# Retention and two MLPs on one core: scores as 64 by 64 products, three chunk buffers in turn, first weights behind chunks 8 and 11

## The chip, the cores and the metric

The kernel runs on one core of a Trainium2 chip. The metric is the device time in microseconds (us) of one execution. Three runs of the kernel before gave 571.97, 572.69 and 572.76 us, a median of 572.69. The profile that is read here is one further execution of 573.28 us, of which the traced span is 571.5 us; the other 1.78 us lie around the span.

## The reference

A retention layer with a decay per head goes into two MLPs with different activations. Cut to what matters:

```python
gamma = 1 - 2 ** (-5 - arange(8))          # one decay per head
for t in range(768):                       # B, H, S, D = 2, 8, 768, 64
    state = gamma * state + einsum('bhd,bhe->bhde', k[:, :, t], v[:, :, t])
    y[:, :, t] = einsum('bhd,bhde->bhe', q[:, :, t], state) / sqrt(64)
x = y as [1536 tokens, 512]
h = x @ w_in;  x = (h * tanh(softplus(h))) @ w_out     # first MLP, 512 -> 2048 -> 512
h = x @ w_in2; out = (h * cos(h)) @ w_out2             # second MLP, same sizes
```

q, k and v are float32; the four weights are float64 and are taken apart on the chip into a high and a low float32 part.

## The kernel before, in words

**Two stages.** The retention runs first, in 12 chunks of 128 tokens (six for each of the two batches). Behind it come the two MLPs, 24 steps of matrix products with 512 moving columns. TensorE goes from the one to the other without a break.

**One chunk of the retention.** Chunk g arrives as two loads of 512 KB on the SP queue (`chunk_loads`, `att_load`): columns 0 to 1023 hold q and k (here "qk half"), columns 1024 to 2047 hold v and the other layout of k ("vk half"). Four groups of products run on TensorE:

- `att_scores` (line 325): 8 products, key by query, per head; 64 rows by 128 columns of the array, in float32. It writes two PSUM tiles, which VectorE masks into `p` (`att_mask`).
- `att_inter` (line 370): 8 products of 64 rows by 64 columns, the state of the chunk before (`st`) with the decayed queries (`qd`).
- `att_update` (line 341): 8 products of 128 rows by 64 columns, which add the chunk (`vd`) to the state. The last chunk of a batch (5 and 11) has none.
- `att_out` (line 381): 8 products of 128 rows by 64 columns, masked scores by v.

Each float32 product is two records (weight load and matmul) in the trace, so a group of 8 products is "x16". The first chunk of a batch (0 and 6) has no `att_inter`.

**Order on TensorE.** It is written by hand: scores(0), a few products with zeros, and then for n = 0 to 11: scores(n+1), inter(n), update(n), out(n). Behind out(11) come the first products of the MLP (`products(11)`, `deal`), line 428.

**The other engines in this stage.** POOL makes `qd` and some `vd`; ScalarE the other `vd` (lists `VD_ACT`), some states `st` (`ST_ACT`) and the high part of x (`att_x_high`); VectorE the masks, the other states and the low part of x.

**The planner.** `Plan` puts every operation in order by costs and dependences written in the kernel. TensorE and SP keep the written order; on the other engines what can start first comes first. `op(..., uses=, new=)` names the buffers that an operation reads or takes.

**Where the chunks lie.** Chunks 0 and 1 lie in a tile of x, 2 to 4 in three buffers `qkv`, 5 to 7 in the three buffers of the output weights, 8 and 9 in two buffers of g, and 10 and 11 in the buffers of chunks 2 and 3. So no load of chunks 2 to 9 waits for a chunk's end.

**First weights.** The weight tile `("i", 0, 0)` of the first MLP is loaded in two halves (here i00a and i00b), `("i", 0, 1)` in two more (i01a, i01b). In the written order of SP i00a stands behind chunk 6, i00b behind chunk 9, and i01a and i01b behind chunk 11. Each half is then taken apart: abs (ScalarE, `w_abs_act`), clamp, exponent, sign (VectorE), high part (ScalarE), low and low part (VectorE). `hold` keeps single steps of this from coming before a named step of the retention.

Of the kernel before, what the change touches and what calls it, by code (L numbers as in the profile page):

```python
# [10 lines left out]
F32 = mybir.dt.float32  # L11
# [13 lines left out]
BLK = 512  # L25
# [7 lines left out]
IN_WO = (5, 6, 7)  # L33
IN_G = (8, 9)
# [142 lines left out]
def retention_two_mlps(ctx: ExitStack, tc: tile.TileContext, qkv, w1i, w1o, w2i, w2o, consts, out):  # L177
# [89 lines left out]
    att = {}  # L267
    vd = {}
# [12 lines left out]
    def att_load(g, lo, hi, eng=nc.sync):  # L281
        if not att:
            t = x_p.tile([128, 2, KD, BLK], F32R, tag="x", name="qkv")
            for n in range(2):
                att[n] = t[:, n].rearrange("p a b -> p (a b)").bitcast(F32)
        elif g in IN_WO and g not in att:
            t = wo_p.tile([128, 2, 2, 512], F32R, tag="wo", name="qkv")
            att[g] = t.rearrange("p a b c -> p (a b c)").bitcast(F32)
        elif g in IN_G and g not in att:
            t = g_p.tile([128, 2, 2, BLK], F32R, tag="g", name="qkv")  # L290
            att[g] = t.rearrange("p a b c -> p (a b c)").bitcast(F32)
        elif g not in att:
            att[g] = att_p.tile([128, 2048], F32, tag="qkv", name="qkv", bufs=3)
        eng.dma_start(out=att[g][:, lo:hi], in_=qkv[g, :, lo:hi])  # L294
# [24 lines left out]
    def att_scores(g):  # L319
        qk = qk_of(g)  # L320
        ss = [ps_p.tile([128, NPAIR, C], F32, tag="s", name="ps_s", bufs=3) for _ in range(2)]
        for a in range(NPAIR):
            for e in range(2):
                h = slice(D * e, D * e + D)
                nc.tensor.matmul(ss[e][:, a, :], qk[h, a, 1, :], qk[h, a, 0, :], start=True, stop=True)  # L325
# [255 lines left out]
    def chunk(g):  # L581
        return ("qkv", max(g, 1))

    def chunk_loads(g, cuts, queue=nc.sync):
        key = chunk(g)
        for lo, hi in zip(cuts, cuts[1:]):
            n = op(
                "SP", (hi - lo) * (0.00142 if g < 3 else 0.00122), att_load, g, lo, hi, queue,
                uses=[key], new=None if key in plan.owner else (key, 3, "x" if g < 2 else "wo" if g in IN_WO else "g" if g in IN_G else "qkv"),
# [5 lines left out]
    def chunk_pre(g):  # L595
        c = g % NCH
        key = chunk(g)
        on_act = g in VD_ACT
        if c + 1 < NCH:
# [3 lines left out]
                    new=None if part else (("vd", g), 2), uses=[key, ("vd", g)],  # L603
# [3 lines left out]
        if c > 0:  # L607
            name, cost, eng = ("DVE", 0.72, nc.vector) if g in QD_DVE else ("POOL", 1.95, nc.gpsimd)
            at["qd", g] = op(
                name, cost, att_qd, g, eng, needs=at["qk", g] + at["decq"], new=(("qd", g), 2), uses=[key]  # L610
# [5 lines left out]
    def chunk_scores(g):  # L616
        s = [("s", g, e) for e in range(2)]
        first = op(None, 0.0, nothing, new=(s[0], 3, "s"))
        at["s", g] = op("PE", 1.05, att_scores, g, needs=at["qk", g] + [first], new=(s[1], 3, "s"), uses=[chunk(g), s[0]])
# [315 lines left out]
```

## Time and profile before

| | us |
|---|---|
| median of three runs | 572.69 |
| profiled execution | 573.28 |
| its span | 571.5 |
| TensorE busy (matmul) in the span | 565.8 |
| VectorE / ScalarE / POOL busy | 382.6 / 230.1 / 97.5 |
| retention, to the first MLP product | 45.65 |

The rows that the prediction rests on stand in a section of their own below. PE is TensorE's matmuls, PEld its weight loads, DVE VectorE, ACT ScalarE, POOL GpSimd, SP the queue that issues the loads. In a timeline, neighbouring instructions of one line are merged: start, length, engine, line, and the count; a bracket gives the idle time ahead and what ended it. A matmul's end in the trace is modelled, so starts are read, and the time of a group of products is taken from its start to the start of the next group. The granted TensorE clock is 1.0 of full speed (2.4 GHz) in all 40 slices of the page.

### The profile page before, as it was taken

The page shows a single profiled execution, that of the slowest core. Times are in us where ns is not written, and L with a number is a line of the kernel's source. Part 1 is how long each engine was busy: PE and PEld are TensorE (multiplying, and loading weights), DVE is VectorE, ACT ScalarE, POOL GpSimd, SP SyncE. Part 2 cuts the span into 40 slices and gives each one's busy share as a digit, 9 for nine tenths or more (in the row PEclk, how much of TensorE's full clock was granted, in tenths as well). Part 3 has the DMA queues.
Part 4 walks back from the last instruction along what each step waited for, and adds up shares of the span by engine and source line. Part 5 has one row for each costly group of instructions (what it writes and reads, how often), then busy time and mean ns, then how long its engine had stood idle before and what let it go on. Part 6 is the DMA issues. An engine that isn't in the chain of part 4 may idle for free.

```text
span 571.5 us, 7260 instructions
## 1 busy us (share of the span) xinstructions
PE 565.8 (99%) x3054; PEld 468.4 (82%) x3054; DVE 382.6 (67%) x416; ACT 230.1 (40%) x284; POOL 97.5 (17%) x74
## 2 busy tenths in 40 slices
PE   8999999999999999999999999999999999999997
PEld 6888888888888888888888888888888888888886
DVE  5779889662375427653487985898498894765462
ACT  3574543422303303214326465465345354354240
POOL 6680001111110301111101111032010312010000
PEclk9999999999999999999999999999999999999999
DMA  8982254422032200412021030304004010000113
GB/s 297 413 335 75 75 210 158 147 75 73 1 131 91 73 1 0 148 73 75 0 75 73 26 123 1 138 10 147 1 0 148 32 41 2 1 1 1 73 38 110
DMA packets 14721, 49.91 MB, mean 87 GB/s; under 512 B 1632, under 2 KB 2016, under 8 KB 14688
## 3 DMA queue, kind: packets, MB, share of 16 engines
q1 hardware_dynamic: 14688, 49.44, 23.4%
q8 instruction: 24, 0.39, 0.3%
q14 instruction: 9, 0.07, 0.0%
HBM read 46.29 MB, written 3.15 MB: 86 GB/s over the span
## 4 chain that ended last, share of the span: by engine, by line
PE 94%; DMA 4%; SPq 1%; ACT 0%; issue 0%; DVE 0%; ACTq 0%
PE ps_h L428 46%; PE ps_o L451 46%; DMA qkv<-qkv_dram 4%; SPq L294 1%; PE ps_y L381 1%; PE ps_y L370 1%; PE ps_s L325 1%; PE ps_u L341 0%; ACT vd L308 0%; ACT x L395 0%; DVE acc L517 0%; SPq L758 0%; ACT st L353 0%; ACTq L308 0%
## 5 line engine op out<-in xcount | busy, mean ns | idle before, releaser
L428 PE MATMUL ps_h<-x,wi 128*128 128x512 f32 x1152 | 264.8, 389 | 0.0
L428 PEld LDWEIGHTS ps_h<-x,wi 128*128 128x128 f32 x1152 | 216.1, 188 | 45.0 <-issue 0.2
L451 PE MATMUL ps_o<-wo,g 128*128 128x512 f32 (+1 forms) x588 | 132.5, 385 | 0.0
L451 PE MATMUL ps_o<-g,wo 128*128 128x512 f32 x576 | 132.3, 389 | 0.0
L451 PEld LDWEIGHTS ps_o<-wo,g 128*128 128x128 f32 x588 | 108.9, 188 | 22.1
L451 PEld LDWEIGHTS ps_o<-g,wo 128*128 128x128 f32 x576 | 108.1, 188 | 22.5
L494 DVE TENSOR_TENSOR g<-mish,g 128x1024 fp32r<-128x1024 f32 x24 | 33.4, 1393 | 59.2 <-ACT g L490 59.2
L262 POOL TENSOR_TENSOR wo<-mag,wo 128x1024 fp32r<-128x1024 f32 x14 | 35.8, 2557 | 212.8 <-ACT wo L248 212.8
L510 DVE TENSOR_TENSOR acc<-ps_o,acc 128x1024 f32<-128x1024 f32 x35 | 42.8, 1222 | 34.6 <-PE ps_o L451 34.4
L262 POOL TENSOR_TENSOR wi<-mag,wi 128x1024 fp32r<-128x1024 f32 x12 | 30.3, 2525 | 193.1 <-ACT wi L248 193.1
L461 ACT ACTIVATE mish<-ps_h 128x1024 f32<-128x1024 f32 (+1 forms) x25 | 24.9, 995 | 95.1 <-PE ps_h L428 95.1
L474 DVE SCALAR_TENSOR_TENSOR turns<-whole,turns 128x1024 f32<-128x1024 f32 x24 | 29.4, 1223 | 44.7 <-ACT whole L470 44.7
L466 ACT ACTIVATE turns<-ps_h,quarter 128x1024 f32<-128x1024 f32 x24 | 26.7, 1114 | 65.4 <-PE ps_h L428 65.1
L239 DVE SCALAR_TENSOR_TENSOR mag<-raw,mag 128x1024 uint32<-128x1024 uint32 (+1 forms) x38 | 42.2, 1110 | 1.1
L483 ACT ACTIVATE turns<-turns 128x1024 f32<-128x1024 f32 x24 | 25.5, 1062 | 34.8 <-DVE turns L480 34.6
L494 DVE TENSOR_TENSOR g<-turns,g 128x1024 fp32r<-128x1024 f32 x24 | 33.2, 1384 | 8.0 <-ACT g L490 8.0
L486 DVE TENSOR_TENSOR turns<-turns,ps_h 128x1024 f32<-128x1024 f32 x24 | 29.2, 1216 | 10.1 <-ACT turns L483 6.8
L254 DVE SCALAR_TENSOR_TENSOR mag<-raw,mag 128x1024 uint32<-128x1024 uint32 x26 | 33.7, 1301 | 0.4
L490 ACT CAST g<-turns 128x1024 fp32r<-128x1024 f32 x24 | 25.1, 1044 | 16.9 <-DVE turns L486 16.9
L248 ACT CAST wi<-mag 128x1024 fp32r<-128x1024 f32 (+1 forms) x20 | 17.5, 876 | 27.3 <-DVE mag L254 22.4
L470 ACT ACTIVATE whole<-turns,magic 128x1024 f32<-128x1024 f32 x24 | 27.7, 1153 | 0.8
L480 DVE TENSOR_SCALAR turns<-turns 128x1024 f32<-128x1024 f32 x24 | 27.0, 1126 | 0.8
(50 smaller groups left out, 330.2 us busy)
## 6 DMA issues: line engine op xcount, KB each, us to landing
qkv<-qkv_dram SPq DMA_DIRECT2D x24, 512.0 KB, 10.1
raw<-w1i_dram SPq DMA_DIRECT2D x16, 512.0 KB, 4.2
raw<-w1o_dram SPq DMA_DIRECT2D x16, 512.0 KB, 4.1
raw<-w2i_dram SPq DMA_DIRECT2D x16, 512.0 KB, 4.0
raw<-w2o_dram SPq DMA_DIRECT2D x16, 512.0 KB, 3.6
out_dram<-acc SPq DMA_DIRECT2D x11, 256.0 KB, 2.1
out_dram<-acc SPq DMA_DIRECT2D x2, 128.0 KB, 1.7
few<-consts_dram SPq DMA_DIRECT2D x1, 146.0 KB, 2.2
```

The lines of the kernel that those rows point to most:

```text
L239: nc.vector.scalar_tensor_tensor(out=a, in0=high, scalar=0xC0000000, in1=a, op0=ALU.bitwise_and, op1=ALU.bitwise_or)
L254: nc.vector.scalar_tensor_tensor(out=w_all_of(it, single)[:, ns], in0=raw_t[it][:, ns, :, 0], scalar=29, in1=mag_t[it][:, ns], op0=ALU.log ...
L262: eng.tensor_sub(out=w[:, :, 1], in0=w_all_of(it, single)[:, ns].bitcast(F32), in1=w[:, :, 0].bitcast(F32))
L428: nc.tensor.matmul(h[:, 0 if h_tag(k) == "s" else f % 2, :], w[:, f % 2, a, kk * 128 : (kk + 1) * 128], x[:, b, kk, :], start=(a + b + kk ...
L451: nc.tensor.matmul(ps, lhs, rhs, start=(n == 0), stop=(n == 3 * GF - 1))
L466: nc.scalar.activation(out=t_t[k], in_=h_t[k], func=AF.Identity, scale=INV_2PI, bias=quarter)
L470: nc.scalar.activation(out=n_t[k], in_=t_t[k], func=AF.Identity, bias=magic)
L474: nc.vector.scalar_tensor_tensor(out=t, in0=n_t[k], scalar=MAGIC, in1=t, op0=ALU.subtract, op1=ALU.subtract)
L480: nc.vector.tensor_scalar(out=t, in0=t, scalar1=-0.5, scalar2=0.5, op0=ALU.max, op1=ALU.min)
L486: nc.vector.tensor_mul(out=t_t[k], in0=t_t[k], in1=h_t[k])
L494: nc.vector.tensor_sub(out=g[:, :, 1, :], in0=t_t[k], in1=g[:, :, 0, :].bitcast(F32))
L510: nc.vector.tensor_add(out=acc, in0=o_t[m * NG + G, j, p], in1=acc)
```

## The change

- **Scores.** Each of the 8 score products is split by its 128 keys into two of 64 rows by 64 columns: 16 products, in the order (rows 0, keys 0), (rows 1, keys 0), (rows 0, keys 1), (rows 1, keys 1) for each pair of heads.
- **Buffers.** Chunks 0 and 1 stay in the tile of x; from chunk 2 on the chunks take three buffers a0, a1, a2 in turn (`HOME`). So the load of chunk g waits for chunk g-3, from chunk 5 on: its qk half for the readers of that chunk's qk half (scores, qd), its vk half for those of the vk half (vd, update, out). The buffers of the output weights and of g hold no chunk any more.
- **First weights.** In SP's order i00a stands behind chunk 8, i00b behind chunk 11 and ahead of i01a.
- **Holds.** Clamp and sign of i00a wait for the masks of chunks 8 and 9 (were 6 and 7); the clamp of i00b waits for the mask of chunk 11 (was 9), its abs for x of chunk 9 (was 6).
- The planner's costs of scores and inter are 0.94 and 0.55 (were 1.05 and 0.62); they order operations and are no measurement.

```diff
--- before.py
+++ after.py
@@ -30,8 +30,7 @@
 GF = 4
 NG = NF // GF
 NCHK = B * NCH
-IN_WO = (5, 6, 7)
-IN_G = (8, 9)
+HOME = ("x0", "x1", "a0", "a1", "a2", "a0", "a1", "a2", "a0", "a1", "a2", "a0")
 H_ATT = {(0, 0, 0): "s", (0, 1, 0): "h0", (0, 0, 1): "y", (0, 1, 1): "h0"}
 VD_ACT = (1, 2, 4, 7, 9)
 ST_ACT = (3, 4, 6, 7, 8, 9)
@@ -265,6 +264,7 @@
 
     x_t = {}
     att = {}
+    homes = {}
     vd = {}
     qd = {}
     state = {}
@@ -279,18 +279,15 @@
         return x_t[m, j]
 
     def att_load(g, lo, hi, eng=nc.sync):
-        if not att:
-            t = x_p.tile([128, 2, KD, BLK], F32R, tag="x", name="qkv")
-            for n in range(2):
-                att[n] = t[:, n].rearrange("p a b -> p (a b)").bitcast(F32)
-        elif g in IN_WO and g not in att:
-            t = wo_p.tile([128, 2, 2, 512], F32R, tag="wo", name="qkv")
-            att[g] = t.rearrange("p a b c -> p (a b c)").bitcast(F32)
-        elif g in IN_G and g not in att:
-            t = g_p.tile([128, 2, 2, BLK], F32R, tag="g", name="qkv")
-            att[g] = t.rearrange("p a b c -> p (a b c)").bitcast(F32)
-        elif g not in att:
-            att[g] = att_p.tile([128, 2048], F32, tag="qkv", name="qkv", bufs=3)
+        home = HOME[g]
+        if g not in att:
+            if home == "x0" and home not in homes:
+                t = x_p.tile([128, 2, KD, BLK], F32R, tag="x", name="qkv")
+                for n in range(2):
+                    homes[f"x{n}"] = t[:, n].rearrange("p a b -> p (a b)").bitcast(F32)
+            elif home not in homes:
+                homes[home] = att_p.tile([128, 2048], F32, tag=home, name="qkv", bufs=1)
+            att[g] = homes[home]
         eng.dma_start(out=att[g][:, lo:hi], in_=qkv[g, :, lo:hi])
 
     def qk_of(g):
@@ -320,9 +317,13 @@
         qk = qk_of(g)
         ss = [ps_p.tile([128, NPAIR, C], F32, tag="s", name="ps_s", bufs=3) for _ in range(2)]
         for a in range(NPAIR):
-            for e in range(2):
-                h = slice(D * e, D * e + D)
-                nc.tensor.matmul(ss[e][:, a, :], qk[h, a, 1, :], qk[h, a, 0, :], start=True, stop=True)
+            for t in range(2):
+                keys = slice(D * t, D * t + D)
+                for e in range(2):
+                    h = slice(D * e, D * e + D)
+                    nc.tensor.matmul(
+                        ss[e][keys, a, :], qk[h, a, 1, keys], qk[h, a, 0, :], start=True, stop=True, skip_group_check=True,
+                    )
         s_t[g] = ss
 
     def att_mask(g, e):
@@ -578,15 +579,16 @@
             for n in range(ns.start, ns.stop):
                 at["w", it, n] = last
 
-    def chunk(g):
-        return ("qkv", max(g, 1))
+    def chunk(g, part):
+        return [(part, g)] + [("qkv", "x")] * (HOME[g][0] == "x")
 
     def chunk_loads(g, cuts, queue=nc.sync):
-        key = chunk(g)
         for lo, hi in zip(cuts, cuts[1:]):
+            half = "qk" if lo < 1024 else "vk"
+            key = chunk(g, half)
             n = op(
-                "SP", (hi - lo) * (0.00142 if g < 3 else 0.00122), att_load, g, lo, hi, queue,
-                uses=[key], new=None if key in plan.owner else (key, 3, "x" if g < 2 else "wo" if g in IN_WO else "g" if g in IN_G else "qkv"),
+                "SP", (hi - lo) * (0.00142 if g < 3 else 0.00122), att_load, g, lo, hi, queue, uses=key,
+                new=None if key[0] in plan.owner else (key[0], 1, half + HOME[g]),
             )
             for part, last in (("qk", 1024), ("v", 1536), ("k", 2048)):
                 if lo < last and hi > last - 512:
@@ -594,20 +596,19 @@
 
     def chunk_pre(g):
         c = g % NCH
-        key = chunk(g)
         on_act = g in VD_ACT
         if c + 1 < NCH:
             at["vd", g] = [
                 op(
                     *(("ACT", 0.98) if on_act else ("POOL", 1.15)), att_vd, g, part, needs=at["v", g] + at["dec"],
-                    new=None if part else (("vd", g), 2), uses=[key, ("vd", g)],
+                    new=None if part else (("vd", g), 2), uses=[*chunk(g, "vk"), ("vd", g)],
                 )
                 for part in range(2 if on_act else 1)
             ]
         if c > 0:
             name, cost, eng = ("DVE", 0.72, nc.vector) if g in QD_DVE else ("POOL", 1.95, nc.gpsimd)
             at["qd", g] = op(
-                name, cost, att_qd, g, eng, needs=at["qk", g] + at["decq"], new=(("qd", g), 2), uses=[key]
+                name, cost, att_qd, g, eng, needs=at["qk", g] + at["decq"], new=(("qd", g), 2), uses=chunk(g, "qk")
             )
 
     def nothing():
@@ -616,7 +617,7 @@
     def chunk_scores(g):
         s = [("s", g, e) for e in range(2)]
         first = op(None, 0.0, nothing, new=(s[0], 3, "s"))
-        at["s", g] = op("PE", 1.05, att_scores, g, needs=at["qk", g] + [first], new=(s[1], 3, "s"), uses=[chunk(g), s[0]])
+        at["s", g] = op("PE", 0.94, att_scores, g, needs=at["qk", g] + [first], new=(s[1], 3, "s"), uses=[*chunk(g, "qk"), s[0]])
         for e in range(2):
             at["p", g, e] = at["p", g] = op(
                 "DVE", 0.71, att_mask, g, e, needs=[at["s", g]] + at["mask"],
@@ -630,7 +631,7 @@
         u, st = ("u", g // NCH), ("st", g)
         at["u", g] = op(
             "PE", 0.52, att_update, g, needs=at["vd", g] + at["k", g] + ([at["st", g - 1]] if c else []),
-            uses=[u, chunk(g), ("vd", g)], new=None if c else (u, 1, "u"),
+            uses=[u, *chunk(g, "vk"), ("vd", g)], new=None if c else (u, 1, "u"),
         )
         at["st", g] = op(
             *(("ACT", 1.0) if g in ST_ACT else ("DVE", 0.43)), att_state, g, needs=[at["u", g]], new=(st, 2), uses=[u],
@@ -639,11 +640,11 @@
     def chunk_inter(g):
         if g % NCH:
             uses = [("st", g - 1), ("qd", g), ("y", g)]
-            op("PE", 0.62, att_inter, g, needs=[at["st", g - 1], at["qd", g]], uses=uses, new=(("y", g), 1, y_tag(g)))
+            op("PE", 0.55, att_inter, g, needs=[at["st", g - 1], at["qd", g]], uses=uses, new=(("y", g), 1, y_tag(g)))
 
     def chunk_out(g):
         y, x = ("y", g), ("x", 0, g // 4)
-        uses = [("p", g), chunk(g), y]
+        uses = [("p", g), *chunk(g, "vk"), y]
         at["y", g] = op(
             "PE", 0.98, att_out, g, needs=[at["p", g]] + at["v", g], uses=uses,
             new=None if y in plan.owner else (y, 1, y_tag(g)),
@@ -795,13 +796,12 @@
 
     at["close"] = op(None, 0.0, close)
     op("PE", 5.5, start_up)
+    op(None, 0.0, nothing, new=(("qkv", "x"), NJ, "x"))
     load = op("SP", 0.4, load_consts, new=("few", 3, "g"))
     cuts = (0, 1024, 2048)
-    for g in range(7):
+    for g in range(9):
         chunk_loads(g, cuts)
-    weight(("i", 0, 0), lambda: [chunk_loads(g, cuts) for g in (7, 8, 9)])
-    for g in (10, 11):
-        chunk_loads(g, cuts)
+    weight(("i", 0, 0), lambda: [chunk_loads(g, cuts) for g in (9, 10, 11)])
     weight(("i", 0, 1))
     plan.given.remove("SP")
     last = op("DVE", 0.85, att_mask_grow, needs=[load], uses=["few"])
@@ -840,13 +840,13 @@
 
     i00, i01 = ("i", 0, 0), ("i", 0, 1)
     for n, what, ns, it in (
-        (6, "clamp", 0, i00), (7, "sign", 0, i00), (11, "dve low", 0, i00),
-        (9, "clamp", 1, i00), (11, "dve low", 1, i00),
+        (8, "clamp", 0, i00), (9, "sign", 0, i00), (11, "dve low", 0, i00),
+        (11, "clamp", 1, i00), (11, "dve low", 1, i00),
     ):
         hold(at[what, it, ns], at["p", n])
     hold(at["sign", i00, 1], at["xl", 9])
     hold(at["act", i00, 0], at["xh", 4])
-    hold(at["act", i00, 1], at["xh", 6])
+    hold(at["act", i00, 1], at["xh", 9])
     hold(at["high", i00, 1], at["st", 10])
     hold(table, at["xh", 10])
     hold(at["act", i01, 0], at["xl", 10])
```

## Rows read from the trace of the kernel before

**Rows 1.** The page: busy us, share of the span, instructions; busy tenths in 40 slices.

```profile
PE 565.8 (99%) x3054; PEld 468.4 (82%) x3054; DVE 382.6 (67%) x416; ACT 230.1 (40%) x284; POOL 97.5 (17%) x74
...
DMA  8982254422032200412021030304004010000113
```

**Rows 2.** The chain that ended last, 0 to 80 us: start, length, what.

```profile
17.44 11.76 DMA qkv<-qkv_dram
...
45.72 32.89 PE ps_h L428 x144
```

**Rows 3.** Timeline of PE: start, length, engine, line, operation, count.

```profile
12.46 1.16 PE L325 MATMUL ps_s<-qkv 64*128 64x128 f32 x16
13.55 0.67 PE L370 MATMUL ps_y<-qd,st 64*64 64x128 f32 x16
14.15 0.69 PE L341 MATMUL ps_u<-vd,qkv 128*64 128x64 f32 x16
14.67 1.04 PE L381 MATMUL ps_y<-p,qkv 128*64 128x128 f32 x16
15.64 1.16 PE L325 MATMUL ps_s<-qkv 64*128 64x128 f32 x16
...
45.65 14.60 PE L428 MATMUL ps_h<-x,wi 128*128 128x512 f32 x63
```

**Rows 4.** Timeline of PEld (weight loads), 12.4 to 15.7 us.

```profile
12.46 0.97 PEld L325 LDWEIGHTS ps_s<-qkv 64*128 64x128 f32 x16 [0.32 <-DMA qkv<-qkv_dram]
13.55 0.42 PEld L370 LDWEIGHTS ps_y<-qd,st 64*64 64x64 f32 x16
14.15 0.55 PEld L341 LDWEIGHTS ps_u<-vd,qkv 128*64 128x64 f32 x16 [0.17 <-ACT vd L308]
14.61 0.86 PEld L381 LDWEIGHTS ps_y<-p,qkv 128*64 128x64 f32 x16
```

**Rows 5.** Timeline of PE, cut at 13.82 and at 13.93 us: the same group.

```profile
13.55 0.45 PE L370 MATMUL ps_y<-qd,st 64*64 64x128 f32 x8
...
13.55 0.56 PE L370 MATMUL ps_y<-qd,st 64*64 64x128 f32 x12
```

**Rows 6.** Timeline of PE, 26.8 to 33 us.

```profile
26.87 1.09 PE L381 MATMUL ps_y<-p,qkv 128*64 128x128 f32 x16
28.05 1.16 PE L325 MATMUL ps_s<-qkv 64*128 64x128 f32 x16
...
30.63 1.16 PE L325 MATMUL ps_s<-qkv 64*128 64x128 f32 x16
32.07 0.99 PE L370 MATMUL ps_y<-qd,st 64*64 64x128 f32 x16 [0.28 <-ACT st L353]
```

**Rows 7.** Timeline of ACT, 29 to 47 us.

```profile
29.28 1.06 ACT L308 ACTIVATE vd<-qkv,cst 128x64 f32<-128x64 f32 x4 [1.93 <-DMA qkv<-qkv_dram]
...
31.68 0.90 ACT L353 ACTIVATE st<-ps_u,cst 128x64 f32<-128x64 f32 x4
...
46.62 0.62 ACT L248 CAST wi<-mag 128x512 fp32r<-128x512 f32 x1
```

**Rows 8.** Windows: stretch, busy us of PE, PEld, DVE, ACT, POOL; PEclk, DMA share, GB/s.

```profile
20.00:23.00 3.00, 3.00 (x64) 2.63 (x64) 1.89 (x3) 2.71 (x10) 2.69 (x5) 1.00 1.02 410
...
41.00:44.00 3.00, 3.00 (x64) 2.56 (x64) 2.37 (x5) 0.56 (x2) 1.58 (x3) 1.00 0.04 18
```

**Rows 9.** Timeline of SP: the last loads of chunks issued.

```profile
26.72 4.09 SPq L294 DMA_DIRECT2D qkv<-qkv_dram  x4
```

**Rows 10.** Issue to landing: line 211 at 48 to 53 us (two halves), then line 294.

```profile
DMA to landing us min/median/max: 3.3/3.8/4.2
...
DMA to landing us min/median/max: 4.9/10.1/12.0
```

**Rows 11.** Timeline of POOL: qd of chunk 2.

```profile
13.36 1.53 POOL L316 TENSOR_TENSOR qd<-qkv,cst 64x256 f32<-64x256 f32 x2
```

**Rows 12.** Waits of PEld from 45 us to the end: us in total, times, longest.

```profile
PEld ps_h L428 <- issue: 0.2, 1, 0.2
```

## Prediction

> **What bounds the kernel now.** I read the page first: TensorE is busy for 99% of the span, the other engines for 67% or less [rows 1]. Then the chain that ended last: a load of a chunk up to 29.2 us, then TensorE without a break, with the first MLP product at 45.7 us [rows 2]. Behind 45 us TensorE's weight loads wait 0.2 us in all [rows 12]: the MLPs are one unbroken run on TensorE, and whatever the retention ends sooner reaches the end one for one, as long as nothing in the MLPs' first steps comes late. So only the time from the first chunk to 45.65 us is in play.
>
> In that stage a chunk is a slot of four groups on TensorE, 12.46 to 15.64 us: scores 1.09, inter 0.60, update 0.52, out 0.97, together 3.18 us [rows 3]. At 12.46 us TensorE still waited for a load [rows 4]; nothing can be gained ahead of that. Behind it, it is TensorE's own pace but for two late starts. Scores of chunk 7 start 1.18 us behind the start of out(5), where 1.02 would do (0.97, and 0.05 for the change of form, below): 0.16 late. Inter(7) starts 1.44 us behind scores(8), where 1.09 would do: 0.35 late, behind a state that ScalarE makes after it stood 1.93 us for the vk half of chunk 7 [rows 6, 7]. The loads run ahead at 410 GB/s with the DMA engines full [rows 8], so 512 KB take 1.28 us and a chunk 2.56.
>
> **Scores, and the inter behind them.** Inter is the nearest row to a product of 64 by 64 with 128 columns. Cut at 13.82 us the group holds 8 records and ends at 14.00, cut at 13.93 it holds 12 and ends at 14.11 [rows 5], and all 16 end at 14.22 [rows 3]: four records, that is two products, per 0.11 us. Its 0.60 are 4 x 0.11 and 0.16 at its edges. Weight loads show the edges: inter's end at 13.97 and update's begin at 14.15, 0.18 later, while out's begin (14.61) before update's end (14.70) [rows 4]. Update and out have one form, inter and update have not; scores and inter have not either (loads end 13.43, begin 13.55). I put 0.05 of the 0.16 at the start and 0.11 at the end.
>
> The new scores are 16 products, 8 x 0.11 = 0.88. They come behind out, of another form, so 0.05 more: 0.93. Inter behind them has the same form and loses its start, 0.55. The pair takes 1.48 where it took 1.69: 0.21 less. The other bound: in the new order every second neighbour uses the same columns of the array, in inter none does. If that delays one group of two products by 0.11, the pair takes 1.59, 0.10 less; and if the split saves nothing at all, 0. I take 0.19, near inter, since the engine, the form and the number of columns are inter's. Behind 12.46 us there are nine such pairs (scores 2 to 6 and 8 to 11), and scores(7), behind which an update comes, saves 0.05. Sum: 9 x 0.19 + 0.05 = 1.76 us. The slot becomes 2.99 us.
>
> **The three buffers.** Before, the last chunk loads were issued at 26.7 to 30.8 us, far ahead [rows 9]. Now the vk half of chunk g+2 waits for out(g-1). All of SP's queue stands behind that wait: the qk half of g+3, and later the weights. A half that is issued alone lands 3.3 us later, and one issued 0.4 behind it took 4.2 [rows 10]; so the next is some 1.28 behind. So the qk half of g+3 is there 3.35 + 1.28 = 4.6 us after out(g-1) ends. TensorE asks for it two slots later, 5.98 us. In the steady state the wait is covered with 1.4 us to spare; half vk has over 2 us more. At the start, chunk 5: its qk half waits for qd(2), which POOL ends at 14.89 us [rows 11]; the queue of loads is then still full, and it lands near 20, for scores(5) at 21.4. Cost nil; without that cover each us of lateness would be one us of TensorE per slot.
>
> **Where it isn't covered.** Chunk 5 has no update and chunk 6 no inter, so slots are short there, and i00a now stands between vk8 and qk9. Let out(4) end at U.
> - vk7 lands at U + 3.4; in the profile it took 2.9 us from such a landing (29.2) to inter(7) (32.07), over vd and the state on ScalarE [rows 6, 7]. So inter(7) can start at U + 6.3. TensorE gets there at U + 0.93 + 0.55 + 1.02 + 1.04 + 0.52 + 0.97 + 0.93 = U + 5.96: 0.34 late, as before (0.35).
> - vk8 waits for out(5), which ends at U + 2.50. With i00a ahead of it qk9 lands 0.05 + 3.35 + 2 x 1.28 = 5.96 later, at U + 8.46. TensorE gets to scores(9) at U + 6.3 + 0.55 + 0.52 + 0.97 = U + 8.34: 0.1 late.
>
> That is 0.45 of new lateness for 0.51 of old. It counts on idle DMA engines. Before, a few per cent of the engines' time went on at 41 to 44 us, 0.04 x 16 = 0.6 of one engine [rows 8]: one engine runs late, and a half has landed when the last of 16 engines has. I take 0.35 us of that into the wait for chunk 9; the bounds are 0 and 0.7. Net of the late starts: +0.3.
>
> **Edits with one answer.** The old buffers of chunks 5 to 9 are free sooner, which nothing waits for [rows 12]. i00b lands behind vk11, which waits for out(8), now ending near 36.4: 36.5 + 3.35 + 1.28 = 41.1 us. Its high part needs abs, clamp, exponent, sign and cast, some 2.9 us by their lengths in the trace, so 44.0 at best; it is wanted when 12 products (12 x 0.23 us) of the first half are through, near 46.9. Before, the cast stood at 46.62, ahead of a need at 48.4 [rows 7]. The cover is 2 to 3 us of those products; if VectorE's masks push the chain further than that, TensorE waits for the rest.
>
> **Sum.** 1.76 - 0.3 = 1.46: the first MLP product near 44.2 us. The profiled execution would go from 573.28 to 571.8; it lies 0.59 above the median, so the median goes from 572.69 to 571.2.
>
> **Rivals.**
> - *A, as above*, 571.2. With the pair at 0.21 less, no late engine and no wait at inter(7), the gain is 2.4 (570.3); with 0.10 and the full 0.7, it is 0.95 + 0.05 - 0.65, about 0.35 (572.3). Chance 0.63.
> - *B, the loads set the pace.* If a half lands L after its release, two slots can't be shorter than L + 1.28. At L = 4.7 the cover is gone, at L = 5.1 the slot is 3.18 again: 572.2 to 573.2. For it: halves in a full queue took 4.9 to 12 us [rows 10]. Against: the queue is empty when a load waits for its buffer. The case that the split saves nothing counts here too (about 572.5). Chance 0.22.
> - *C, slower: the small products go one at a time.* Scores, update and out, whose neighbours share rows or columns of the array, take one product per 0.11 to 0.14 us with 128 columns; only inter, whose neighbours share neither, takes two per 0.11 [rows 3, 5]. If sharing is what counts, 16 products take 16 x 0.11 = 1.78: the pair is 0.64 longer, nine times, and the other scores 0.69: 6.4 us, 579. It turns to a loss when a product costs over (1.69 - 0.55) / 16 = 0.071 us. Against: the rates also fit the share of the array that a product fills, halves for those three and quarters for inter, and the new ones fill quarters. Chance 0.12.
> - *D, slower: a price per instruction.* 16 more records per chunk at inter's 0.0275 us each are 0.44, eleven times, 4.8 us: 577.5. Against: these 0.0275 are inter's whole time per record, so there is no room for a price on top. Chance 0.03. The Trainium skill, TensorEngine Tiling, "Instruction Overhead", states about 60 cycles of overhead for each matmul and warns of tiling a small dimension further; as an estimate from that page, 16 x 25 ns would be 0.4 us more per chunk.
>
> **How the numbers follow.** About 0.2%, 1.15 us (571.54), is what a measurement of this kernel can tell from no change. A's centre is only 0.35 beyond it, and its spread 0.6, so some 0.7 of A is faster and the rest no change. Faster 0.46, same 0.38, slower 0.16 (C, D, a little of B). The range takes in A and B with the runs' 0.4: 570.0 to 573.1.
>
> **What would show it.** Right: scores to inter 0.93, inter to update 0.55, slots of 3.0 us, no weight-load pause between scores and inter, first MLP product at 44 to 44.5. SP shows waits for out(g-3); PE a wait of 0.3 to 0.8 at scores(9) and one at inter(7). Wrong: scores near 1.8 (C) or 1.35 (D); waits for loads at every scores from chunk 6 on (B); a wait behind 45.65 for i00b.

## The result and the profile after

The kernel after takes 576.3 us in the median (four runs, 575.46 to 577.35), the kernel before beside it 572.4; the ratio is 1.0069, 95% interval 1.0048 to 1.0091. It is slower by 3.9 us where 1.5 us less was forecast. The profiled execution took 575.65 us with a span of 573.7, 2.2 more than the span of before; the granted clock is 1.0 in all slices, as before.

The timeline of PE of the kernel after, from the first scores of the stretch to the MLP (start, length, engine, line, operation, count; in the bracket the idle time ahead and what ended it):

```profile
15.61 1.09 PE L324 MATMUL ps_s<-qkv 64*64 64x128 f32 x30 [0.36 <-DMA qkv<-qkv_dram]
...
18.66 1.10 PE L324 MATMUL ps_s<-qkv 64*64 64x128 f32 x32
19.58 0.62 PE L371 MATMUL ps_y<-qd,st 64*64 64x128 f32 x16
20.13 0.50 PE L342 MATMUL ps_u<-vd,qkv 128*64 128x64 f32 x9
20.91 0.39 PE L342 MATMUL ps_u<-vd,qkv 128*64 128x64 f32 x6 [0.27 <-issue]
...
30.68 0.87 PE L324 MATMUL ps_s<-qkv 64*64 64x128 f32 x20
32.29 0.54 PE L324 MATMUL ps_s<-qkv 64*64 64x128 f32 x10 [0.74 <-issue]
...
35.79 1.10 PE L324 MATMUL ps_s<-qkv 64*64 64x128 f32 x32 [0.92 <-DMA qkv<-qkv_dram]
...
37.78 0.28 PE L382 MATMUL ps_y<-p,qkv 128*64 128x128 f32 x1
38.73 1.09 PE L382 MATMUL ps_y<-p,qkv 128*64 128x128 f32 x15 [0.68 <-issue]
...
47.30 3.03 PE L429 MATMUL ps_h<-x,wi 128*128 128x512 f32 x12
50.56 11.63 PE L429 MATMUL ps_h<-x,wi 128*128 128x512 f32 x50 [0.23 <-ACT wi L247]
```

Set it against [rows 3]. Scores and inter take 18.66 to 20.13 = 1.47 us where they took 1.69: the products themselves gained what was forecast. But the groups are now broken in the middle. A group of one kind, whose inputs are all there, stops after 9 of 16 records of update(3), after 20 of 32 of scores(8), after one of out(8), and what ended the pause is "issue": no engine and no DMA that the profile knows of. A fourth such break stands in scores(6), where the weight loads stand still for 0.33 us, and loads come late, most of all that of scores(9) at 35.79. The first MLP product is at 47.30 us, 1.65 later than in [rows 3], and the MLP itself has a break at 50.56, where it waits for a weight.

The account from the scores of chunk 2 to the MLP (12.46 to 45.65 = 33.19 us before, 12.21 to 47.30 = 35.09 after), each pause as the time by which the broken group and the one behind it, which it draws out, are longer than in a slot without a pause:

| | us |
|---|---|
| before | 33.19 |
| old lateness gone: scores(7) 0.16, inter(7) 0.35 at its start and 0.32 in itself | -0.83 |
| nine pairs shorter by 0.22, scores(7) by 0.05 | -2.03 |
| pauses: update(3) 0.54, scores(6) 0.40, scores(8) 1.16, out(8) 0.99 | +3.09 |
| loads late: scores(3) 0.53 with the pair behind it, scores(7) 0.14, scores(9) 0.99 | +1.66 |
| sum (measured 35.09) | 35.08 |

The 0.32 in inter(7) of before is read from its start at 32.07 [rows 6] to that of the group behind it, 0.92 where 0.60 would do:

```profile
32.99 0.69 PE L341 MATMUL ps_u<-vd,qkv 128*64 128x64 f32 x16
```

With half a microsecond more at 50.56 (the twelve products of the first half would have ended at 50.06) this is the 2.2 us of the spans. The other three runs of after were 0.2 shorter to 1.7 us longer than its profiled one, the runs of before lay within 0.8, so the medians differ by more than the two traces. One execution of another kernel, the small products below, took 2041.6 us and is counted nowhere.

From the page of after, the busy row and a DMA queue (transfers, MB, share of 16 engines):

```profile
PE 564.8 (98%) x3246; PEld 467.7 (82%) x3246; DVE 382.1 (67%) x416; ACT 230.3 (40%) x284; POOL 97.0 (17%) x74
...
q8 instruction: 25, 0.41, 0.3%
```

q8 is the queue that the page calls "instruction": 25 transfers where the page of before has 24, each of 16,384 bytes by its records. TensorE has twice 3246 = 6492 weight loads and matmuls where it had 6108 [rows 1]: a float32 product is four records, two weight loads and two matmuls, so 8 products more are 32 instructions more per chunk. A slot of before holds 130 instructions of TensorE, one of after 162.

The waits of SP of after up to 60 us (line waited for: us in total, times, longest), and behind them the chunk loads' time from issue to landing:

```profile
SPq L291 <- PE ps_y L382: 18.7, 7, 4.1
...
SPq L291 <- PE ps_s L324: 4.6, 1, 4.6
```

```profile
DMA to landing us min/median/max: 3.6/5.8/11.7
```

SP waits for out and scores of the chunk three back, as forecast; a half then lands 3.6 us after its issue at best, where [rows 10] has 3.3.

### The profile page after: what moved, and what is told of

The parts are those of the page before. It is cut to its first block, busy times and chain, and to the rows that moved or that the text cites. A ratio compares the mean times of both kernels' runs of the same rounds, so it can differ in the third digit from the quotient of the medians.

```text
span 573.7 us, 7647 instructions
## 1 busy us (share of the span) xinstructions
PE 564.8 (98%) x3246; PEld 467.7 (82%) x3246; DVE 382.1 (67%) x416; ACT 230.3 (40%) x284; POOL 97.0 (17%) x74
## 4 chain that ended last, share of the span: by engine, by line
PE 93%; DMA 4%; SPq 1%; POOL 1%; ACT 1%; issue 0%; DVE 0%; POOLq 0%
PE ps_o L452 46%; PE ps_h L429 45%; DMA qkv<-qkv_dram 3%; DMA raw<-w1i_dram 1%; PE ps_s L324 1%; SPq L291 1%; PE ps_y L382 1%; POOL qd L313 0%; PE ps_u L342 0%; PE ps_y L371 0%; POOL qd L310 0%; ACT L456 0%; ACT mag L215 0%; ACT x L396 0%; ACT wi L247 0%
## 5 line engine op out<-in xcount | busy, mean ns | idle before, releaser
L238 DVE SCALAR_TENSOR_TENSOR mag<-raw,mag 128x1024 uint32<-128x1024 uint32 (+1 forms) x38 | 40.3, 1060 | 1.1
L232 DVE TENSOR_SCALAR mag<-mag 128x1024 uint32<-128x1024 uint32 (+1 forms) x38 | 27.0, 710 | 1.1
```

Source lines behind the costliest of these rows:

```text
L232: nc.vector.tensor_scalar(out=a, in0=a, scalar1=3, scalar2=0x3FFFFFF8, op0=ALU.logical_shift_left, op1=ALU.bitwise_and)
L238: nc.vector.scalar_tensor_tensor(out=a, in0=high, scalar=0xC0000000, in1=a, op0=ALU.bitwise_and, op1=ALU.bitwise_or)
```

## The experiments

Two explanations stand at first. *Blocks*: TensorE's instructions come in blocks over the DMA engines that also carry the chunks, and the split scores use them up faster than they come while loads fill the engines. *Gate*: the three buffers let loads go too late. Beside each run stands the kernel before on the same chip, 572.1 to 572.4 us.

**The split alone.** The kernel before with the new loop in `att_scores`; the old buffers and weight order stay.

```diff
-            for e in range(2):
-                h = slice(D * e, D * e + D)
-                nc.tensor.matmul(ss[e][:, a, :], qk[h, a, 1, :], qk[h, a, 0, :], start=True, stop=True)
+            for t in range(2):
+                keys = slice(D * t, D * t + D)
+                for e in range(2):
...
```

> Only the split of the scores (and the two planner costs that go with it); buffers, weight order and holds as before. Theory F (TensorE's instructions arrive in blocks of 256, and 32 more per chunk make it ask for blocks faster than they come through the full loads): pauses of 0.3 to 1.0 us at every 256th instruction between 18 and 41 us, as in the changed kernel, the first MLP product between 44.6 and 46.5 us, time within 1.5 us of before. Theory G (the loads that now wait for their buffers land late, and the split itself is sound): no such pauses, first MLP product near 43.5 us, time near 570.3.

Measured 577.54 us, ratio 1.0095 [1.008, 1.011]: 5.4 us slower, worse than the whole change and than either theory had it. Timeline of PE of this kernel:

```profile
21.51 0.39 PE L345 MATMUL ps_u<-vd,qkv 128*64 128x64 f32 x6 [1.33 <-issue]
...
27.70 0.54 PE L327 MATMUL ps_s<-qkv 64*64 64x128 f32 x9 [1.10 <-issue]
...
34.47 0.55 PE L327 MATMUL ps_s<-qkv 64*64 64x128 f32 x10 [1.44 <-issue]
...
40.66 1.09 PE L385 MATMUL ps_y<-p,qkv 128*64 128x128 f32 x15 [1.42 <-issue]
...
49.22 21.15 PE L432 MATMUL ps_h<-x,wi 128*128 128x512 f32 x92
```

No wait for a load is among these pauses. They come at the same instructions as those of after (behind record 9 of update(3), 23 of scores(6), 20 of scores(8), 1 of out(8)). Numbered from 0 in TensorE's stream of both traces, the first instruction behind each is 705, 961, 1217 and 1473 (its weight loads, matmuls and sequencer instructions counted): 256 apart. The records of q8 show a transfer start at 19.04, 25.27, 32.12 and 38.36 us and take 1.0 us; TensorE goes on 1.3 to 1.5 us behind its end. From one end of a pause to the next it is 6.2, 6.8 and 6.2 us. By the measure of the account above the pauses cost 6.6 us from scores(3) to the MLP, against 1.8 that the pairs save and 0.8 of old lateness: 4.0 in sum, as the two traces differ there (33.98 against 30.01).

**The buffers alone.** The kernel after with the old `att_scores` and the two old costs.

> The three buffers, the weight order and the holds of the change, with the scores as before. Theory F: no pause at 256-instruction borders, and the loads of chunks land soon enough for a slot of 3.18 us, so the first MLP product is at 45.5 to 46.3 us, time within 1 us of before. Theory G: waits for loads at the scores of chunks 7 to 9 and a wait for the second weight half, first MLP product past 46.5 us and its second half later still, time 574 to 577.

Measured 575.91, ratio 1.0066 [1.0049, 1.0083]: 3.8 us slower. Timeline of PE:

```profile
28.09 1.16 PE L322 MATMUL ps_s<-qkv 64*128 64x128 f32 x16 [0.26 <-DMA qkv<-qkv_dram]
...
31.52 1.16 PE L322 MATMUL ps_s<-qkv 64*128 64x128 f32 x16 [0.79 <-DMA qkv<-qkv_dram]
...
35.33 1.16 PE L322 MATMUL ps_s<-qkv 64*128 64x128 f32 x16 [0.55 <-DMA qkv<-qkv_dram]
...
39.12 1.16 PE L322 MATMUL ps_s<-qkv 64*128 64x128 f32 x16 [0.54 <-DMA qkv<-qkv_dram]
...
47.16 0.43 PE L367 MATMUL ps_y<-qd,st 64*64 64x128 f32 x3 [0.77 <-issue]
...
48.55 21.64 PE L425 MATMUL ps_h<-x,wi 128*128 128x512 f32 x94
```

Here the waits are for loads, at one scores after another, 2.14 us together; one pause without a releaser is left, at instruction 1473. By the measure of the account the late loads cost 2.8 us and that pause 1.2: whole scores stop at a border too where three buffers draw the loads out. The transfer of its block started 4.4 us behind the border before it. So the parts alone cost 5.4 and 3.8 us, the one by pauses at borders, the other mostly by loads, and together 3.9, not 9.2.

**No loads in the way.** The kernel after and the one above, without the loads of chunks 5 to 11 (one execution each):

```diff
+        if g < 5:
             eng.dma_start(out=att[g][:, lo:hi], in_=qkv[g, :, lo:hi])
```

> The changed kernel with the loads of chunks 5 to 11 left out (they work on the data of chunks 2 to 4, so the output is not the reference's); the weight halves are still loaded. Theory F: with the loads gone blocks of instructions come in time, no pause at 256th instructions behind 20 us, slots of 2.97 us, first MLP product near 42.8 us. If the pauses stay, they are not from the loads, and the first product is at 44.5 or later. Theory G alone also expects 42.8.

> The control of the run before: the three buffers and the weight order with the scores as before, and the loads of chunks 5 to 11 left out (output not the reference's). Slots of 3.18 us, no pauses, first MLP product near 44.9 us: 1.9 to 2.1 us behind the split one. If the split saved nothing without loads, the two would be equal.

Measured 572.0 with the split (span 570.2), 571.28 with whole scores (span 569.4). Timelines of PE, with the split and with whole scores, and windows with the split (stretch; busy us of PE, PEld, DVE, ACT, POOL; clock, DMA share, GB/s):

```profile
21.77 0.39 PE L343 MATMUL ps_u<-vd,qkv 128*64 128x64 f32 x6 [1.64 <-issue]
...
23.02 1.10 PE L325 MATMUL ps_s<-qkv 64*64 64x128 f32 x32
...
33.97 1.10 PE L325 MATMUL ps_s<-qkv 64*64 64x128 f32 x32
...
36.93 1.10 PE L325 MATMUL ps_s<-qkv 64*64 64x128 f32 x32
...
44.47 25.91 PE L430 MATMUL ps_h<-x,wi 128*128 128x512 f32 x113
```

```profile
20.79 1.16 PE L323 MATMUL ps_s<-qkv 64*128 64x128 f32 x16
...
43.61 26.63 PE L426 MATMUL ps_h<-x,wi 128*128 128x512 f32 x116
```

```profile
14.00:20.00 6.00, 5.18 (x143) 4.44 (x139) 3.95 (x8) 2.75 (x11) 4.56 (x6) 1.00 1.03 421
...
26.00:32.00 6.00, 6.00 (x166) 5.31 (x168) 3.83 (x7) 3.92 (x15) 4.17 (x6) 1.00 0.01 4
```

The only pause left is the one whose block came while the last loads still ran (421 GB/s). Behind it the same instructions run with no pause, in slots of 33.97 to 36.93 = 2.96 us; with whole scores the slot is 3.18. From scores(5) to the MLP the split takes 23.02 to 44.47 = 21.45 us, whole scores 20.79 to 43.61 = 22.82: 1.4 us less. So the split is worth what was forecast, where nothing loads. Ahead of that it lost more, by the pause of 1.64 and a late load of chunk 3: its first MLP product is at 44.47, where 42.8 was expected, and that of whole scores at 43.61, where 44.9 was. And a block's transfer starts 1.15 us behind the end of a pause here (21.77 to 22.92), under full loads 3.8 to 4.4 us behind it (21.51 to 25.27 in the split alone).

**Rows of 2 KB.** If a block stands behind the packets of the loads, smaller packets might let it through. Each half was cut in two again, `cuts = (0, 512, 1024, 1536, 2048)`: in the split alone, in the kernel before and in the kernel after.

> The split of the scores alone (as e1_scores), with every chunk load cut in two: rows of 2 KB in place of 4 KB, 48 loads of 256 KB. In e1_scores a block of 256 instructions took 5.9 to 6.8 us from the pause before, and the pauses summed to 5.6 us. Theory F with the wait in a queue (a block's transfer stands behind the load packets already queued at its DMA engine): half as much ahead of it, pauses under 0.8 us each, time 573 to 575.5. Rival (a block comes slowly whenever the engines are full, however the loads are cut): pauses as in e1_scores, time 577 to 578.5.

> Control: the kernel before with every chunk load cut in two. Its 256 instructions take two slots, 6.2 to 6.4 us, so it should hardly pause in either theory: 571.5 to 573 us, a little less if the first chunks' qk halves come sooner; 574 or more if loads of 2 KB rows are slower as such.

> The whole change with every chunk load cut in two. Theory F with the wait in a queue: the pauses (2.4 us in all) go to under 1.2; the waits for chunk 9 and for the second weight half stay or shrink a little, since part of a chunk is released sooner: 573.5 to 575.5. Rival: as the change, 575.5 to 577.5.

Measured 577.72 (1.0092 [1.0077, 1.0107]), 576.17 (1.0066 [1.0049, 1.0082]) and 578.81 (1.0114 [1.0099, 1.0129]). In the first the pauses are 0.92, 1.38, 1.55 and 1.69, about as with 4 KB rows. From 20 to 44 us its loads move only 324 to 392 GB/s, at a DMA share of 0.99 to 1.06: neither smaller packets nor a lower rate bring the block sooner while the engines stay full. The second is a miss of its own: the kernel before loses 3.8 us by the cut alone, at waits for loads. Its timeline of PE:

```profile
29.15 1.30 PE L325 MATMUL ps_s<-qkv 64*128 64x128 f32 x16 [1.08 <-DMA qkv<-qkv_dram]
...
40.62 1.16 PE L325 MATMUL ps_s<-qkv 64*128 64x128 f32 x16 [1.73 <-DMA qkv<-qkv_dram]
```

Its loads move 307 to 387 GB/s from 20 to 44 us, against 405 to 416 in the same stretch of before as long as loads last. In the third the pauses of after grow, where under 1.2 us in all was expected (0.74, 1.04, 1.49, 0.30 and, at one border more, 0.67), and loads for scores(8) and scores(9) come late.

**Old weight order.** The kernel after with i00a and i00b at their old places and the old holds.

```diff
-    for g in range(9):
+    for g in range(7):
         chunk_loads(g, cuts)
-    weight(("i", 0, 0), lambda: [chunk_loads(g, cuts) for g in (9, 10, 11)])
+    weight(("i", 0, 0), lambda: [chunk_loads(g, cuts) for g in (7, 8, 9)])
+    for g in (10, 11):
+        chunk_loads(g, cuts)
```

> The change with the first weights in their old places (i00a behind chunk 6, i00b behind chunk 9) and the old holds; the split and the three buffers stay. If the late second weight half is what the change loses at the MLPs' start, its wait of 0.5 us there goes, and the wait for chunk 9 falls by a half load (1.3 us), while one of 1.3 us can come at chunk 7 and 10: time 574.5 to 576. Theory F: the pauses at 256th instructions stay, 2 to 3 us in all, so it stays slower than before by over 1.5 us. Theory G alone: back to 572 to 573.

Measured 578.17, 1.0109 [1.0087, 1.0131]: about 2 us more than the change and more than expected, though no wait for i00b is left in the MLP. Its largest wait is 2.12 us for a load at scores(7), ahead of which i00a now stands:

```profile
30.05 1.29 PE L324 MATMUL ps_s<-qkv 64*64 64x128 f32 x32 [2.12 <-DMA qkv<-qkv_dram]
```

The new places of the weights aren't the loss: with three buffers the old ones are worse.

**The count alone.** Sixteen products with one column ahead of each inter of the kernel before add as many instructions per chunk as the split (16 weight loads, 16 matmuls) and leave scores whole; a twin leaves out the loads of chunks 5 to 11 as above.

```diff
+        for _ in range(16):
+            nc.tensor.matmul(ps[0:64, 0, 0, 0:1], zero[0:64, 0:64], zero[0:64, 0:1], start=True, stop=True, skip_group_check=True)
```

> The kernel before, scores and buffers untouched, with 16 products of one column and zeros ahead of each of the ten inter groups (they are overwritten by the inter products): as many instructions more per chunk as the split brings, 32, and hardly any array work. Theory F (the count of instructions is what stalls TensorE while the loads fill the DMA engines): idle stretches that no engine explains at every 256th instruction, as in e1_scores 6.2 to 6.8 us apart, 0.5 to 1.5 us each; together with the tiny products' own 0.3 to 0.9 us per chunk the time is 578 to 582. Rival (the form of the new products, not their count, stalls it): no such stretches, only the tiny products' own time.

> The control for e10_tiny: the same tiny products in e5_whole_noload (three buffers, whole scores, the loads of chunks 5 to 11 left out, so the output is not the reference's). It shows the tiny products' own time per chunk against e5_whole_noload. Theory F: no stretch of idling at 256th instructions behind 22 us. If there are such stretches without loads, theory F is wrong on what makes a block late.

> The kernel of e10_tiny once more, for its profile (the one taken showed an execution in which TensorE ran several times slower from start to end). Without loads the tiny products took 0.49 us per chunk. Theory F: 164 instructions per slot of 3.67 us, so 256 take 5.7 us against the 6.2 to 6.8 of a block under full loads: idle stretches of 0.3 to 1.0 us at 256th instructions between 20 and 42 us, which e12_tiny_noload doesn't have. Rival (form, not count): none there.

Three runs took 577.54 to 579.58 (1.0106 [1.009, 1.0122]); the profile is of a further execution of 577.91. Without loads it took 577.01, with slots of 3.67 us: the small products cost 0.49 us per chunk of their own. That is most of the 6 us, and the slots become so long that 256 instructions take some 5.8 us. Without loads there is no pause behind 22 us; with them one for a block is left, at instruction 1217:

```profile
36.33 0.93 PE L383 MATMUL ps_y<-p,qkv 128*64 128x128 f32 x13 [0.33 <-issue]
```

So whole scores with more instructions pause at a border too, but at one of four and for 0.33 us, less than expected. The test is weak, since its products take the time in which a block comes.

**The split in fewer chunks.** In the kernel before, in odd chunks only, and, with `g > 9` for `g % 2`, in chunks 10 and 11 only:

```diff
-        for a in range(NPAIR):
-            for e in range(2):
+        if g % 2:
+            for a in range(NPAIR):
+                for t in range(2):
...
+        else:
+            for a in range(NPAIR):
+                for e in range(2):
...
```

> The kernel before with the scores split in the odd chunks alone: half of the additional instructions. Theory F: a block still takes 6.2 to 6.8 us while the loads run, against 5.4 to 5.7 us of work for 256 instructions: pauses of 0.5 to 1.1 us, some 2.5 to 3.5 us in all in place of 5.6; 573.5 to 576. Rival (a fixed price per split group): the mean of before and e1_scores, 574.8, without regard to where the borders lie.

> The kernel before with the scores split only in chunks 10 and 11, whose groups run when the loads come to their end (40 us). Theory F: no pause is added, the two pairs save 0.2 us each: 571.9 against 572.3, which a measurement hardly tells from no change. With a pause at the border near 39 us it would be 0.5 to 1.5 us slower.

Measured 573.53 (1.0021 [1.0012, 1.003]) and 572.34 (1.0002 [0.9993, 1.0011]). The first has pauses of 0.30, 0.26 and 0.67 us, again 256 instructions apart (961, 1217, 1473); the profile puts the last one down to TensorE's own out(9):

```profile
28.57 0.65 PE L328 MATMUL ps_s<-qkv 64*64 64x128 f32 x11 [0.30 <-issue]
...
34.95 0.55 PE L328 MATMUL ps_s<-qkv 64*64 64x128 f32 x11 [0.26 <-issue]
...
41.38 1.10 PE L328 MATMUL ps_s<-qkv 64*64 64x128 f32 x32 [0.67 <-PE ps_y L391]
```

From one to the next it is 6.4 us, as in the split alone (6.2 to 6.8): the block sets the time there, whatever TensorE could do. TensorE idles 1.2 us in them, less than expected. By the account's measure they cost 2.1, of which the shorter scores of the odd chunks give back 0.9; the run loses 1.2, where all of the split loses 5.4. The split where hardly any load is left gains two pairs, 0.4 us by the sum, which the runs can't tell from nothing.

**A fourth buffer.** HOME with one buffer of the output weights as the fourth in turn, on the buffers alone (whole scores) and on the kernel after (split):

```diff
-HOME = ("x0", "x1", "a0", "a1", "a2", "a0", "a1", "a2", "a0", "a1", "a2", "a0")
+HOME = ("x0", "x1", "a0", "a1", "a2", "wo", "a0", "a1", "a2", "wo", "a0", "a1")
...
+            elif home == "wo" and home not in homes:
+                t = wo_p.tile([128, 2, 2, 512], F32R, tag="wo", name="qkv")
+                homes[home] = t.rearrange("p a b c -> p (a b c)").bitcast(F32)
```

> e2_buffers (whole scores) with a fourth chunk buffer, in the place of one buffer of the output weights: each load is released one slot earlier. In e2_buffers a half landed 3.7 to 5.7 us after its release, where 4.7 for the second of two is the most that the slots cover. Theory W (the release is too late for that): with 3.2 us more the waits at the scores of chunks 8 to 10 go, first MLP product at 45.3 to 46.3 us, time 572 to 573.5. Rival (the new weight order or the order of the other engines costs it): waits elsewhere, time stays at 574.5 to 576.5.

> The whole change with a fourth chunk buffer. Theory F: the loads run further ahead and fill the DMA engines for longer, so the pauses at 256th instructions grow from 2.4 us towards the 5.6 of e1_scores while the waits for chunks go: 575 to 577.5, no better than the change. Rival (both losses come from the late release): 570.5 to 572.

Measured 572.15 (0.9998 [0.9989, 1.0008]) and 577.61 (1.0098 [1.0077, 1.0118]). With whole scores the loss of three buffers is gone, the pause at 1473 with it, and no scores waits for a load behind 12.7 us; from scores(2) to the MLP it takes 32.36 us, before without its lateness of 0.83. With the split the pauses are back, larger than in after. Timelines of PE, whole and split:

```profile
12.68 1.16 PE L325 MATMUL ps_s<-qkv 64*128 64x128 f32 x16 [1.02 <-DMA qkv<-qkv_dram]
...
45.04 25.23 PE L428 MATMUL ps_h<-x,wi 128*128 128x512 f32 x110
```

```profile
21.87 0.39 PE L345 MATMUL ps_u<-vd,qkv 128*64 128x64 f32 x6 [1.64 <-issue]
...
40.08 1.09 PE L385 MATMUL ps_y<-p,qkv 128*64 128x128 f32 x15 [2.32 <-issue]
...
45.69 0.27 PE L327 MATMUL ps_s<-qkv 64*64 64x128 f32 x1 [0.54 <-issue]
```

By the account's measure its pauses cost 6.2 us, and late loads at scores(3) and scores(9) 1.3. In one table, us against the kernel before that was timed beside it:

| | whole scores | split scores |
|---|---|---|
| old buffers and weight order | 0 | +5.4 |
| four buffers | -0.2 | +5.3 |
| three buffers | +3.8 | +3.9 |

The split costs over 5 us where the loads run on, and no more than the intervals can tell where the gate holds them back. The windows of the split with four buffers, and behind them two of after, suggest why (columns as above):

```profile
20.00:26.00 6.00, 4.36 (x110) 3.79 (x106) 2.59 (x5) 2.98 (x13) 4.85 (x8) 1.00 0.83 302
26.00:32.00 6.00, 5.98 (x152) 4.96 (x149) 3.94 (x7) 4.79 (x17) 2.70 (x4) 1.00 0.88 270
32.00:38.00 6.00, 4.84 (x125) 4.15 (x125) 4.19 (x8) 2.94 (x10) 4.16 (x6) 1.00 1.03 391
```

```profile
14.00:20.00 6.00, 5.64 (x158) 5.04 (x152) 4.41 (x9) 3.21 (x13) 4.70 (x7) 1.00 0.81 322
20.00:26.00 6.00, 5.73 (x143) 4.70 (x135) 3.31 (x7) 4.17 (x16) 3.47 (x5) 1.00 0.90 289
```

Its large pauses end at 21.87 and 40.08, each behind a stretch with the DMA engines full (1.03 from 14 to 20 us and from 32 to 38); at the borders between, with a share of 0.83 and 0.88, TensorE stands 0 and 0.26 us, and 0.54 at the one behind 40.08. In the split alone the share is 1.02 or 1.03 up to 38 us and every border costs over a microsecond; in after it is 0.81 and 0.90 ahead of the pauses of 0.27 and 0.33, then 1.00 and 1.03 ahead of 0.74 and 0.68. So the gaps that the gate leaves seem to let blocks through, and TensorE, when it pauses, asks later for the loads that are late. The share alone doesn't settle it: in the buffers alone the transfer of the block for 1473 started 4.4 us behind the border before it, with a share of 0.87 from 38 to 44 us. That the two losses cover each other in this way is read from these traces and not shown; no run changed the gaps alone.

## Why the prediction was wrong

**What held.** Where TensorE neither pauses nor waits for a load, it keeps the forecast pace. The pair takes 1.47 (1.48 in the sum), scores(7) 1.04, a slot without pauses 2.96 (2.99). Rival C, products of 64 by 64 one at a time, and rival D, a price per instruction, are both out: without loads a slot is 0.22 shorter with eight more products in it. That the split alone took D's 577.5 us is chance. The estimate after the Trainium skill's "Instruction Overhead" (TensorEngine Tiling), 0.4 us more per chunk, is likewise not seen in the split. SP's waits for the chunk three back, and TensorE's at scores(9), came where they were said to come; the one at inter(7) did not, since TensorE stood at a border just ahead of it. Two readings were off without turning the result: the old lateness was 0.83 us and not 0.51, and A's smallest gain counts 0.05 twice (0.30, not 0.35).

**The step that failed first: "it is TensorE's own pace but for two late starts".** The costs under "Scores, and the inter behind them" were counted in TensorE's time per product, and they came; the supply of its instructions had no term at all, in the sum or in a rival. The price per instruction in rival D was put into TensorE, where there is none; it lies in the blocks. What the profile of before shows of it: the page's q8 line, which the prediction doesn't draw on, and DMA engines full at 20 to 23 us [rows 8]. A slot of 3.18 us holds 130 instructions there, so 256 last 6.3 us, near what a block needs under full loads in the split alone (6.2 to 6.8). The kernel before stood near that limit without a pause to show it: its block transfers from 14 to 37 us ended 1.8 to 3.8 us ahead of their borders, where TensorE of the split alone went on 1.3 to 1.5 us behind a transfer's end. The split, 162 instructions per 2.97 us, asks for a block each 4.7. By the account's measure this cost 3.1 us in the profiled execution of after and 6.6 in that of the split alone.

The Trainium skill, Runtime: NRT & Kernel Launch, "Instruction fetch mechanics", says that instructions come in 16 KiB blocks of 256 over a DMA queue of the sequencer's own. The trace agrees with both figures. It also says that crossing a block's border is "mostly hidden"; here it is hidden without loads, and with them, where the stream asks too soon, TensorE idles 0.26 to 2.32 us at it. The rule was at hand and not weighed.

**The second: the three buffers.** "3.35 + 1.28 = 4.6 us after out(g-1) ends" was taken from two halves on idle engines [rows 10]. In after the first half behind a release took 3.6 to 4.5 us for chunks 5 to 7 and 4.8 to 6.1 for 8 to 11, and qk9 6.67, with the last of the 16 engines 0.7 to 1.8 us behind the first. By rival B's own rule the cover is gone at L = 4.7, so the halves from chunk 8 on are beyond it. That "the queue is empty when a load waits for its buffer" did not hold: vk7 was issued at 25.27, and qk7 ahead of it landed at 28.02. This is rival B, at the chance of 0.22; but its price went only up to "at L = 5.1 the slot is 3.18 again", at most 0.5 us above before, and with whole scores three buffers cost 3.8. The fourth buffer, one slot more of cover, takes all of it back, so the late release is shown as the cause, of the late loads and of the pause at 1473. How much of a landing is the half ahead and how much the engines' uneven ends is not settled.

**The third: i00b.** "The cover is 2 to 3 us" counted on a landing at 41.1. Released by out(8), which the pauses and the late load had moved to 39.7, and 6.56 us from issue to landing, it came at 46.85; the timeline of ACT of after:

```profile
46.85 0.67 ACT L215 ACTIVATE mag<-raw 128x512 f32<-128x512 f32 x1 [3.43 <-DMA raw<-w1i_dram]
...
49.89 0.62 ACT L247 CAST wi<-mag 128x512 fp32r<-128x512 f32 x1
```

The chain of 2.9 us that was counted took 3.7 here, and 12 products end at 50.06: 0.5 us of TensorE, by the mechanism that was named and a landing that was over five late.

**The chances.** Slower had 0.16, nearly all of it for C, which was wrong. That loads set the pace was thought of and priced only up to the old slot, since the split was taken to give its gain in any case. What stays open: why a block takes 6.2 to 6.8 us under loads, and up to 8.0 in other runs, though its own transfer takes 1.0, and why other executions of after are up to 1.7 us longer than the one profiled.

## What to carry to other kernels

Where an edit raises the number of instructions on a busy engine, divide 256 by their rate in each stage and set that time beside the DMA traffic of the same stage: a stage that runs its instructions out as fast as blocks arrive loses what faster products gain. When a buffer is taken away, take the landing time behind a release from loads in the same traffic and not from idle engines, and ask for its worst and not its best. Two losses at one resource may hide each other, so undo each part alone before one is blamed.

## What was not expected of the hardware

- TensorE stops at borders of 256 instructions while loads run, if it uses the instructions up sooner than a block comes: 0.26 to 2.32 us idle at a time, most at a DMA share of 1.0 (whether at 410 GB/s or at 324 to 392). A block then took 6.2 to 6.8 us in the split alone, and up to 8.0 elsewhere (27.35 to 35.37 in after with rows of 2 KB). Without loads the same stream has no pause, and the kernel before, with 6.3 us for 256, has none at 405 to 416 GB/s.
- Chunk loads in rows of 2 KB instead of 4 KB moved 307 to 387 GB/s instead of 405 to 416 and cost the unchanged kernel 3.8 us.
- Sixteen one-column products with zeros (16 weight loads, 16 matmuls) cost 0.49 us per chunk; the split adds as many of both, with 128 columns each, and made the slot 0.22 us shorter.
